# Placing the eight fetches of the next block's turned rows among the leaves of the second layer

## Chip, cores and metric

The kernel runs on one core of one Trainium2 chip. The metric is the device time of one execution in microseconds (us). TensorE (PE) does matmuls, VectorE (DVE), ScalarE (ACT) and GpSimd (POOL) do elementwise work, and SyncE (SP) issues nearly all DMA transfers from one queue in order. Each engine runs its own instructions in program order, and semaphores make it wait for data of other engines.

## The reference

Performer attention for 8 batches, 8 heads, 576 positions and 64 dimensions gives `x` of shape (8, 576, 512), and a Fourier mixing block with an MLP follows. All data is float32.

```python
X = np.fft.fft(x, axis=1)
X = np.fft.fft(X, axis=2)
mixed = np.real(X).astype(np.float32)
u = x + mixed
mu = np.mean(u, axis=-1, keepdims=True)
var = np.mean((u - mu) ** 2, axis=-1, keepdims=True)
un = (u - mu) / np.sqrt(var + 1e-06)
ch = np.maximum(un @ w_ch1, 0.0) @ w_ch2
return (u + ch).astype(np.float32)
```

`w_ch1` is 512 x 2048 and `w_ch2` is 2048 x 512. The 8 x 576 = 4608 rows of `u` are the tokens of the MLP.

## The kernel before

**Stages.** The first part of the program does attention and mixing and writes the rows `u` to memory (`us`). The first 512 tokens go through the MLP there, in 4 plain tiles. The other 4096 tokens are 8 blocks of 512 (j = 0 to 7), and the late part of the program is these 8 blocks. Each block has a first layer (`first_of`, matmuls at line 1310) and a second layer (`product_of`, matmuls at line 1490). Both use a recursive scheme with 7 products in place of 8 for a 2 x 2 split, so sums of operands are formed first: `tt` from the normalised rows (`block_norms`, line 1171), `hs` from the hidden rows (line 1377) and `sums` inside a product (line 1457).

**The second layer.** It runs seven products in the order `ORDER = (1, 2, 4, 5, 6, 7, 3)`, and each product has seven leaves in the order of line 1383, `PARTS = (1, 2, 5, 6, 3, 7, 4)`. A leaf is four float32 matmuls in the source, eight matmul instructions in the trace, and needs one tile `wl` of 256 KB that SyncE loads from the prepared weights `w2l` (`loads_w2`, line 1393). There are 12 `wl` buffers; 49 leaves make one second layer. What a leaf leaves in PSUM is saved by ACT or added by DVE, and these steps are named: `p1`, `p5`, `u2` are saved (line 1465), `c11`, `c12`, `c22` are added (line 1470), and `read` marks the last leaf of a product. Leaves 1, 2 and 4 multiply hidden rows (or `hs`) directly, leaves 5, 6, 3 and 7 multiply `sums`.

**The next block's rows.** While block j - 1 is in its first layer, the rows of block j are loaded, normalised (`norm_of`) and transposed in blocks of 32 on DVE (`by_blocks`); the transposed rows go to memory as `turned[j, h]`, for two halves h = 0 and 1. When block j - 1 has used its own normalised rows for the last time, their four buffers (`slab`) come free. Then `fetched(j, h, dst)` brings the turned rows back into `unT`: four DMAs of 128 KB for each half, each into 32 partitions (line 988). This happens for j = 1 to 7, so 56 fetches in all; block 0 takes another way, with transposes on PE. After the fetches `block_norms` forms the sums `tt`, four DVE instructions at line 1171, and the first layer of block j can begin when the second layer of j - 1 is nearly done.

**What sets the order.** The program is written out by a planner (`Listing.run`). Each stream of work (`late_turns`, `late_norms`, `halves`, `loads_w2`, `weight_sums`) yields `Step`s with an engine, an estimated time, events that must have been made before (`after`), an event that it makes, buffers that it takes and gives, and a `bias`. The planner always takes the step that could begin first by its own estimates, plus its bias, and emits its instructions. So an `after` event sets the place of an instruction in its engine's order. On the chip an instruction waits for what it reads and overwrites, and not for such an event by itself. For transfers the planner counts `kb` against a rate of 190 KB per us, and `late` as the delay from issue to landing. Here the fetch of a half is one `Step` of 1.7 us on SP that emits four DMAs in a row, as soon as the buffers are free and the turned rows are in memory.

Of the kernel before, what the change touches and what calls it, by code (L numbers as in the profile page):

```python
# [35 lines left out]
PE, ACT, DVE, POOL, SP, NONE = "pe", "act", "dve", "pool", "sp", "none"  # L36
# [244 lines left out]
def kernel(  # L281
# [39 lines left out]
    TB = 512  # L321
# [26 lines left out]
    mlpp = early.enter_context(tc.tile_pool(name="mlp", bufs=2))  # L348
# [612 lines left out]
    def events_of(tt):  # L961
        return tuple(sorted({("us", r // S) for t in tt for r in (P * t, P * t + P - 1)}))
# [4 lines left out]
    turned = {}  # L967
# [12 lines left out]
        nc.sync.dma_start(t[:, :, k], w[:].rearrange("p g d q -> p g (d q)"))  # L980

    def fetched(j, h, dst):
        yield Step(
            SP, 1.7, 3.0, after=(("turned", j, 2 * h), ("turned", j, 2 * h + 1)),
            makes=("unT", j, h), kb=330,
        )
        for g in range(4):
            nc.sync.dma_start(
                dst[Q * g : Q * g + Q].rearrange("q (b k) d t -> q b (k d t)", k=2),
                turned[j, h][:, g].rearrange("(b q) k n -> q b (k n)", q=Q),  # L990
            )
# [148 lines left out]
    def sums_right(b11, b12, b21, b22, t1, t2, t4):  # L1140

        return (
            (t1, b12, b11, ALU.subtract),
            (t2, b22, t1, ALU.subtract),
            (b12, b22, b12, ALU.subtract),
            (t4, b21, t2, ALU.subtract),
        )
# [3 lines left out]
    def block_norms(j, pool):  # L1151
        t0 = (NPLAIN * TP + TB * j) // 128
        yield Step(NONE, take=("slab",) * 4, after=events_of(range(t0, t0 + TB // 128)) + ("converted",))
        un = unTs[j] = [slabs.tile([128, HT // Q, NDC, Q], F32, name="unT2", tag="slab") for _ in range(2)]
        tt = [slabs.tile([128, 2, HT // Q, D2, Q], F32, name="tt", tag="slab") for _ in range(2)]
        tts[j] = tt[0][:, 0], tt[0][:, 1], tt[1][:, 0]
        for i in range(TB // 128):
            h, k = divmod(i, HT // 128)
            if pool is mlpp:
                dst = un[h][:, 4 * k : 4 * k + 4].rearrange("p g d q -> p d g q")  # L1160
                yield Fork(norm_of(j, t0 + i, i, pool, dst))
            elif not k:
                yield Fork(fetched(j, h, un[h]))
        parts = TB // 128 if pool is mlpp else 2
        yield Step(NONE, after=tuple(("unT", j, i) for i in range(parts)), bias=1.54)
        ops = sums_right(
            un[0][:, :, 0:D2], un[1][:, :, 0:D2], un[0][:, :, D2:NDC], un[1][:, :, D2:NDC], *tts[j]
        )
        for i, (o, l, r, op) in enumerate(ops):
            yield Step(DVE, 0.6, makes=("tt", j) if i == 3 else None, port=True, bias=-0.49)  # L1170
            nc.vector.tensor_tensor(out=o, in0=l, in1=r, op=op)
# [89 lines left out]
    def pairs(start):  # L1261
# [9 lines left out]
        [first(), loads(), loads_v(), load_tables(), frames(), plain_norms(), mixing()]  # L1271
        + [pairs(i) for i in range(NS)]
        + [w2_parts(), weight_sums((0,)), block_norms(0, mlpp), plain(), weights(), warm()],
        PICKS,
    )
# [317 lines left out]
    def late_norms():  # L1593
        for j in range(1, NTB):
            yield from block_norms(j, late)
# [36 lines left out]
```

## Time and profile before

| | us |
|---|---|
| median of 3 runs | 1165.73 |
| lowest and highest run | 1164.71, 1167.06 |
| the profiled execution | 1174.67 |
| its span, first to last instruction | 1172.2 |
| first layers of the blocks, one PE piece each of 168 matmuls | 36.26 |
| second layer of block 7, one PE piece of 368 matmuls | 41.10 |

The span is taken on the profiled execution, which is longer than the runs without a profile. PE stands for matmuls and PEld for TensorE's weight loads, which overlap them. "SPq" is SyncE's queue of DMA issues. In waits, "A <- B: 3.1, 5, 1.4" says that A waited for B for 3.1 us in total, 5 times, 1.4 us at most. In the chain of waits the work that ended last is followed back from the end: a piece "DMA wl<-w2l" goes from the issue of a load to its landing, and the instruction after it was released by that landing. The late part begins at about 424 us in the span, and a block takes about 93 us of it.

### The profile page before, as it was taken

To read this page: it belongs to the slowest core of one execution; us is meant where nothing else is said; L and a number is where in the kernel's file an instruction comes from. 1 tells how busy PE (TensorE), PEld (TensorE's weight loads), DVE (VectorE), ACT (ScalarE), POOL (GpSimd) and SP (SyncE) were. 2 spreads that over 40 slices of the span, in tenths; PEclk is the share of its full clock that TensorE was granted. 3 is DMA by queue.
4 is the path that set the end of the run, shared out by engine and by line. 5 is a ranking of instruction groups with operands and counts; after the bars stand their busy time and mean duration, and the time that the engine had idled before them with its cause. 6 is when DMAs were issued, how large, how long until landed. Compare 5 with 4: busy or idle time off the path is not lost.

```text
span 1172.2 us, 31328 instructions
## 1 busy us (share of the span) xinstructions
PE 1153.5 (98%) x12437; PEld 1032.9 (88%) x12437; DVE 754.7 (64%) x1573; ACT 436.8 (37%) x1485; POOL 430.4 (37%) x496
## 2 busy tenths in 40 slices
PE   8999999999999999999999999999999999999998
PEld 7888888779777868998998998898999899899898
DVE  5999999986676655744754664573573574474255
ACT  6998898866444212122112212212212212221211
POOL 2433444455472106225225324413513512522421
PEclk8999999999999999999999999999999999999999
DMA  7866765665662254873783593694495396388055
GB/s 218 224 188 186 240 181 178 203 210 163 207 196 101 77 162 139 263 264 85 222 278 112 172 308 99 152 317 141 112 319 190 82 290 231 83 258 263 35 166 203
DMA packets 167217, 220.34 MB, mean 188 GB/s; under 512 B 50080, under 2 KB 81056, under 8 KB 167072
## 3 DMA queue, kind: packets, MB, share of 16 engines
q1 hardware_dynamic: 166576, 218.09, 60.7%
q8 instruction: 98, 1.61, 0.6%
q14 instruction: 47, 0.39, 0.1%
q10 hardware_dynamic: 496, 0.26, 0.1%
HBM read 179.24 MB, written 43.25 MB: 190 GB/s over the span
## 4 chain that ended last, share of the span: by engine, by line
PE 88%; DMA 5%; DVE 4%; ACT 2%; SPq 1%; issue 1%; DVEq 0%
PE banks L1310 33%; PE banks L1490 27%; PE banks L1099 5%; PE banks L606 5%; PE banks L1122 4%; PE banks L512 4%; DMA wl<-w2l 3%; PE banks L640 2%; PE banks L687 2%; PE banks L849 2%; PE banks L799 1%; ACT e L566 1%; DVE nmx L549 1%; DMA kq<-in_k_dram 1%; PE banks L809 1%; PE banks L860 1%
## 5 line engine op out<-in xcount | busy, mean ns | idle before, releaser
L1490 PE MATMUL banks<-wl,sums 128*128 128x128 f32 x1792 | 217.4, 275 | 0.0
L1490 PEld LDWEIGHTS banks<-wl,sums 128*128 128x128 f32 x1792 | 208.6, 192 | 0.0
L1296 DVE CUSTOM_DVE_ANT_0 hid<-banks,s 128x256 f32<-128x256 f32 x192 | 80.9, 424 | 188.8 <-PE banks L1310 188.8
L566 ACT ACTIVATE e<-banks,nmx 128x128 f32<-128x128 f32 x576 | 165.3, 434 | 23.2 <-DVE nmx L549 22.4
L1324 ACT ACTIVATE s<-banks 128x256 f32<-128x256 f32 x192 | 73.7, 384 | 259.0 <-PE banks L1310 259.0
L1310 PE MATMUL banks<-unT,w 128*128 128x256 f32 x704 | 166.3, 379 | 0.0
L1310 PEld LDWEIGHTS banks<-unT,w 128*128 128x128 f32 x704 | 133.2, 190 | 18.3 <-issue 0.5
L1530 POOL TENSOR_TENSOR ur<-ur,part 128x512 f32<-128x512 f32 x32 | 47.3, 1479 | 267.1 <-ACT part L1523 187.0
L1465 ACT ACTIVATE s<-banks 128x128 f32<-128x128 f32 x168 | 46.6, 278 | 256.7 <-PE banks L1490 220.3
L1310 PE MATMUL banks<-tt,w1s 128*128 128x256 f32 x512 | 126.3, 379 | 0.0
L1310 PEld LDWEIGHTS banks<-tt,w1s 128*128 128x128 f32 x512 | 97.0, 190 | 13.7 <-DVE hid L1296 0.4
L1490 PE MATMUL banks<-wl,hid 128*128 128x128 f32 x768 | 100.0, 276 | 3.2 <-DMA wl<-w2l 3.1
L1470 DVE TENSOR_TENSOR part<-banks,s 128x128 f32<-128x128 f32 x168 | 49.0, 292 | 83.4 <-PE banks L1490 82.2
L549 DVE TENSOR_REDUCE nmx<-banks 128x8 f32<-128x1024 f32 (+1 forms) x96 | 89.3, 951 | 19.7 <-PE banks L606 15.5
L1490 PEld LDWEIGHTS banks<-wl,hid 128*128 128x128 f32 x768 | 94.0, 192 | 6.0 <-DMA wl<-w2l 4.5
L606 PE MATMUL banks<-om,kqT 64*64 64x128 f32 (+1 forms) x2088 | 80.6, 278 | 1.9 <-ACT kv L656 1.2
L1310 PE MATMUL banks<-unT,w1s 128*128 128x256 f32 x320 | 79.5, 379 | 0.0
L606 PEld LDWEIGHTS banks<-om,kqT 64*64 64x64 f32 (+1 forms) x2088 | 65.8, 140 | 13.3 <-issue 4.3
L1490 PE MATMUL banks<-wl,hs 128*128 128x128 f32 x576 | 75.1, 275 | 0.5 <-DVE part L1470 0.4
L1490 PEld LDWEIGHTS banks<-wl,hs 128*128 128x128 f32 x576 | 70.1, 192 | 1.2 <-DVE part L1470 0.6
L1377 POOL TENSOR_TENSOR hs<-hid,hs 128x256 f32<-128x256 f32 x64 | 50.1, 784 | 57.2 <-issue 37.1
L1310 PEld LDWEIGHTS banks<-unT,w1s 128*128 128x128 f32 x320 | 60.4, 190 | 8.7
(128 smaller groups left out, 1914.6 us busy)
## 6 DMA issues: line engine op xcount, KB each, us to landing
wl<-w2l SPq DMA_DIRECT2D x392, 256.0 KB
raw<-in_moe_w_ch_dram SPq DMA_DIRECT2D x32, 512.0 KB
kq<-in_k_dram SPq DMA_DIRECT2D x32, 288.0 KB
kq<-in_q_dram SPq DMA_DIRECT2D x32, 288.0 KB
vd<-in_v_dram SPq DMA_DIRECT2D x32, 288.0 KB
u<-us SPq DMA_DIRECT2D x36, 256.0 KB
ur<-us SPq DMA_DIRECT2D x36, 256.0 KB
out_dram<-ur SPq DMA_DIRECT2D x34, 256.0 KB
```

Source lines behind the costliest of these rows:

```text
L512: nc.tensor.transpose(ps[:, (j - j0) * 128 : (j - j0 + 1) * 128], src(j), ident[:])
L549: nc.vector.tensor_reduce(nmx[:, :, 0:num], pps[:, :, 0 : MF * num].rearrange("p b (c m) -> p b c m", m=MF), axis=AX.X, op=ALU.max, negate ...
L566: nc.scalar.activation(out=e[:, c + (i if num == 1 else 0), :], in_=pps[:, i, MF * c : MF * c + MF], func=AF.Exp, bias=nmx[:, i, c : c + 1],)
L606: nc.tensor.matmul(pps[cols, c, MF * m : MF * m + MF], lhsT=kqT[rows, j, cols], rhs=om2[rows, :],)
L1099: nc.tensor.matmul(hp[:, 0:TP], lhsT=w1[:, dc, 128 * fc : 128 * fc + 128], rhs=unTs[key][:, dc, :], start=(dc == 0), stop=(dc == NDC - 1),)
L1296: nc.vector._custom_dve(TENSOR_ADD_SAT, out=o, in0=ps, in1=sb, s0=FMAX, s1=0.0)
L1310: nc.tensor.matmul(ps[:, 0:HT].rearrange("f (b q) -> f b q", q=Q), lhsT=left(dc), rhs=right(dc), start=start and dc == 0, stop=(dc == D2 - 1),
L1324: nc.scalar.activation(out=s[:], in_=ps[:, 0:HT], func=AF.Copy)
L1377: nc.gpsimd.tensor_tensor(out=o, in0=l, in1=r, op=op)
L1470: nc.vector.tensor_tensor(out=part[:, t, 128 * m : 128 * m + 128], in0=ps[:, 0:128], in1=saved[with_][:], op=ALU.add,)
L1490: nc.tensor.matmul(ps[:, 0:128], lhsT=left[:, f], rhs=wls[j, i, n][:, f], start=start and f == 0, stop=(f == 3), skip_group_check=True,)
L1530: eng.tensor_tensor(out=o, in0=o, in1=other, op=ALU.add)
```

## The change

Each of the four fetches of a half becomes a `Step` of its own, with its own event and with one more `after` event. For the first half these events are the first save, the second save, an addition and the last leaf of product 1 of the second layer of block j - 1; for the second half an addition, the third save and another addition of product 2, and the first save of product 4. The estimate of one fetch is 0.47 us on SP, 3.4 us until it has landed and 82 KB, where four together had 1.7 us, 3.0 us and 330 KB. The sums `tt` are planned after all eight events. The transfers themselves are not changed.

```diff
     def fetched(j, h, dst):
-        yield Step(
-            SP, 1.7, 3.0, after=(("turned", j, 2 * h), ("turned", j, 2 * h + 1)),
-            makes=("unT", j, h), kb=330,
-        )
-        for g in range(4):
+        at = ((1, "p1"), (1, "p5"), (1, "c12"), (1, "read")) if h == 0 else ((2, "c11"), (2, "u2"), (2, "c22"), (4, "p1"))
+        for g, (i, what) in enumerate(at):
+            yield Step(
+                SP, 0.47, 3.4,
+                after=(("turned", j, 2 * h), ("turned", j, 2 * h + 1), (("second", j - 1, i), what)),
+                makes=("unT", j, 4 * h + g), kb=82,
+            )
             nc.sync.dma_start(
                 dst[Q * g : Q * g + Q].rearrange("q (b k) d t -> q b (k d t)", k=2),
                 turned[j, h][:, g].rearrange("(b q) k n -> q b (k n)", q=Q),
...
-        parts = TB // 128 if pool is mlpp else 2
+        parts = TB // 128 if pool is mlpp else 8
         yield Step(NONE, after=tuple(("unT", j, i) for i in range(parts)), bias=1.54)
```

## The prediction

> **What bounds the kernel now.** I read the page first, then the chain of waits in order of time, then the waits of PE and of SyncE's queue, and at last timelines and stretches of one second layer.
>
> ```profile
> PE 1153.5 (98%) x12437; PEld 1032.9 (88%) x12437; DVE 754.7 (64%) x1573; ACT 436.8 (37%) x1485; POOL 430.4 (37%) x496
> ```
>
> PE is busy 98% of the span, so a change can gain only where PE stands still, or where its matmuls are spaced out. The chain shows where that is in the second layers:
>
> ```profile
> 567.09 1.80 PE banks L1490 x16
> 570.94 5.40 DMA wl<-w2l
> 576.39 32.42 PE banks L1490 x288
> ...
> 659.84 41.31 PE banks L1490 x368
> ...
> 1125.18 41.10 PE banks L1490 x368
> ```
>
> The columns are start, length and what ran. Block 7's second layer (1125.18) has no next block to fetch, and its 368 matmuls take 41.10 us without a break. I take that as the undisturbed length. From the first long L1490 piece to the next L1310 piece the other stages of this view last: block 0 474.35 to 516.06, 41.71; block 1 567.09 to 608.81, 41.72; block 2 41.31; block 3 752.18 to 794.55, 42.37; block 4 845.58 to 887.27, 41.69; block 5 938.30 to 981.11, 42.81; block 6 1032.14 to 1074.15, 42.01. Less 41.10 each that is 0.61 + 0.62 + 0.21 + 1.27 + 0.59 + 1.71 + 0.91 = **5.92 us**. The DMA pieces of the chain (5.40 here, 4.96 to 6.71 in six stages) are not lost time: they run under PE's own work, and only their last part is waited for. The waits say who is late:
>
> ```profile
> PE banks L1490 <- DMA wl<-w2l: 3.1, 5, 1.4
> ...
> PEld banks L1490 <- DMA wl<-w2l: 4.5, 7, 1.6
> ...
> SPq L1393 <- DMA unT<-turned: 9.5, 34, 0.6
> ```
>
> PE and its weight loads (which overlap) wait for a `wl` load, and SyncE's queue, which issues these loads, waits 34 times for a fetch to land before it can issue the next load. SyncE's timeline of block 1 shows why:
>
> ```profile
> 566.25 0.32 SPq L1393 DMA_DIRECT2D wl<-w2l  x1
> 566.62 1.85 SPq L988 DMA_DIRECT2D unT<-turned  x4
> 568.57 0.38 SPq L1393 DMA_DIRECT2D wl<-w2l  x1
> 569.05 1.80 SPq L988 DMA_DIRECT2D unT<-turned  x4
> 570.94 10.69 SPq L1393 DMA_DIRECT2D wl<-w2l  x14
> ```
>
> The load issued at 570.94, behind all eight fetches, is the one whose landing ends the stall before 576.39. Two things delay it: the issue of the fetches (1.85 + 1.80 us) and their bytes. The stretches of the same stage give the rates:
>
> ```profile
> 569.00:573.00 4.00, 4.00 (x38) 4.00 (x38) 4.00 (x7) 1.11 (x4) 0.49 (x1) 1.00 1.03 215
> ...
> 577.00:581.00 4.00, 4.00 (x38) 4.00 (x38) 3.28 (x7) 0.56 (x2) 0.00 (x0) 1.00 1.05 386
> ```
>
> After the bounds and the length come the busy us of PE, its weight loads, DVE, ACT and POOL; the last two columns are the busy share of the DMA engines and GB/s. The engines are full in both; with loads alone they move 386 GB/s, with fetches among them 215. The third-last column is the granted clock, 1.00 throughout, so the clock plays no part.
>
> **What the change does to each queue.** No instruction is added or removed: the 56 fetches stay 56 of 128 KB, on the same queue. What moves is their place in SyncE's order, and behind them the four DVE instructions at L1171. The new `after` events are places in the planner's order, not waits on the chip: a fetch still waits there only for its source, its destination and the queue.
>
> *SyncE.* The first fetch keeps its place, because the event (1,"p1") lies before the stage and the slabs come free only at its beginning. Seven fetches go behind later leaves. By block 1's PE timeline (a leaf is 8 matmuls, 40 in 4.63 us less the overlap, about 0.89 us, and the leaves of products 1, 2 and later 4 alternate) I put the events at some 3, 4, 7, 8, 12, 13 and 14 us after the stage begins. So load 15 (the one of 570.94) is issued when its buffer comes free, the end of the fourth leaf, about 568.9, which is 2.0 us earlier. Load 14 comes 0.5 us earlier. Seven fetch issues of 0.45 us go between loads that are needed only some 9 us after their issue. In that window this queue holds nothing but loads; the stores come at the stage's end.
>
> *DMA time.* A load of 262 KB at 386 GB/s takes 0.68 us. A fetch alone is not shown. From below it costs 131 KB at 386 GB/s, 0.34 us. From above: from the issue of load 13 (566.25) to the landing of load 15 (576.34) there are 10.1 us, less three loads, over eight fetches, 1.0 us. I take 131 KB at 215 GB/s, 0.61 us, since that stretch is mostly fetches. In the new order at most two fetches stand ahead of load 15 in place of eight: 6 x 0.61 = 3.7 us less of queue (2.0 with the lower price, 6.0 with the upper). With the earlier issue it lands 4.0 to 8.0 us sooner than now; the greatest whole loss of one stage is 1.71. The stall is gone at every price.
>
> Over the 13.4 us of the first fifteen leaves the engines must now carry fifteen loads and eight fetches: 10.2 + 4.9 = 15.1 us (12.9 to 18.2). A backlog of 1.7 us (none to 4.8) grows slowly, and twelve buffers of 0.89 us stand against it. Leaves after that use 0.89 us for 0.68 of load, so it drains 0.2 us a leaf.
>
> A rule of the Trainium skill speaks against sending the fetches singly: "SBUF — State Buffer", section "The DMA setup-cost knee", gives every DMA some 2 us that do not depend on its size and advises the largest transfers. By that page's formula my estimate for one fetch is 2.3 us and for eight 18.4 us, instead of 4.9; here 14 loads are issued in 10.69 us, one in 0.76, so the trace does not bear it out where DMAs overlap.
>
> *VectorE.* The four L1171 instructions (the timeline of block 3 has them at 763.72 to 766.5, 0.69 us each, 2.75 in all) need all eight fetches. Now they run 12 us after their stage begins, in a stretch where DVE has slack; then they come when the last fetch is planned to land, 14 + 0.5 + 3.4 to 5 us, some 19 us after the stage's beginning. Their users, the next block's first matmuls with `tt`, start 42 us after it, so 20 us of cover are left. What they may push aside on DVE is the work of the fourth product:
>
> ```profile
> 769.78 0.68 DVE L1457 TENSOR_TENSOR sums<-hs 128x512 f32<-128x512 f32 x1
> ...
> 774.04 1.76 DVE L1457 TENSOR_TENSOR sums<-hs 128x512 f32<-128x512 f32 x1
> ```
>
> These feed leaves 5, 6, 7 and 3 of product 5. In the stretches of 4 us of this block DVE is busy 3.04 us from 768 and 3.90 from 772, then 2.63 and 2.04. So up to 2.75 us of delay is worked off by about 780. PE has three products open at a time, and leaves 1 and 2 of the next ones need no sums: three to four leaves, 2.7 to 3.6 us, can stand in. Cost on the path: nothing by that cover, up to 2.75 - 0.89 = 1.9 us a stage without it. I book 0.1 us a stage, 0.7 in all, for PE's order shifting around them.
>
> *The sum.* Gain between 4.0 us (what the stages lose over the best fetching one, 41.31: 5.92 - 7 x 0.21 = 4.45, less the 0.40 of block 0, whose late load belongs to a later product) and 5.92; I take 5.1, less 0.7 for DVE: **4.4 us**. The profiled execution took 1174.67 us, of which 1172.2 are span; it would become 1170.3 and 1167.8. It is 8.9 us longer than the median of the runs shown, 1165.73. The part that I change is a sum of waits, not a share of the whole, so I take the same 4.4 us off the median: **1161.3 us**.
>
> **The rivals.**
>
> *The wait moves to a later load.* Block 0 is the example: its stall before 489.02 ends with a load issued at 482.18 that took 6.71 us, long after the fetches were issued. If every stage kept such a loss (0.61 x 7 = 4.3 us), 1.6 us would be gained: 1164.1. Also, the profiled execution may stall more than the others do. For it: the backlog is spread, not removed. Against: the total queue ahead of such a load is smaller, since two or three fetches now come after it.
>
> *Slower: the L1171 group lands on DVE's full stretch.* The place is 19 to 22 us into the stage. It decides as soon as the last fetch's planned landing falls after the sums of product 5 are due and PE has no leaf without sums. The price is 1.9 us x 7 = 13.0 less the 4.4 gained plus the 0.7 already booked: +7.9, 1173.6. For it: 3.90 of 4 us busy, and the planner weighs those four ahead of the sums (bias -0.49 against -0.39). Against: no PE wait for sums now, and the planner can put other leaves there.
>
> *A single fetch is dear.* At 1.0 us or more each, fetches keep the loads from the engines for 8 us in 13, and the early loads of product 4 are late again by about 1 us in each stage: 7 us instead of 5.92, 1166.8. The fixed cost of the page named above would work in this direction. Against it stand the 14 loads in 10.69 us.
>
> *The change does nothing:* the loads in between hold the queue up so that the fetches still bunch. Then it is 1165.7. I count it with the first rival.
>
> **How the numbers follow.** Three runs spread over 0.2%, so 0.2% (2.3 us) is what a measurement can tell from no change. My forecast has a chance of 0.57, its own range 1159.0 (everything gained and a little more order) to 1163.3. The moved wait has 0.19, the dear fetch 0.04: both within 0.2%. The DVE collision, or another unlucky order of the planner of the same kind, has 0.20; half of it, at a smaller price than the full 1.9 us a stage, ends below 1170. So faster 0.57, same 0.23, slower 0.20. The range 1159.0 to 1170.0 leaves out the dear half of the last case and a little at each end of the first.
>
> **What would show it.** Right: SyncE's timeline has fetches singly between loads over some 13 us; the chain has no `wl` pieces in the second layers; PE's wait for `wl` falls below 1 us; the seven stages last 41.1 to 41.4 us; L1171 sits some 19 us into each stage and PE waits for no `sums`. Wrong: stages that still last over 41.6 with a `wl` load named (moved wait), PE waits at L1490 for `sums` or `part` (collision), or a first layer that starts late for `tt`.

## The result and the profile after

The changed kernel takes 1196.63 us (median of 6 runs, 1191.39 to 1198.82), the kernel before 1166.04 us beside it (6 runs, 1164.71 to 1167.06). The ratio is 1.0255, with a 95% interval from 1.0229 to 1.0281: 30.6 us slower. The prediction said 1161.3. The profiled execution after has a span of 1195.8 us. Lines of the source are two further down after the change (1490 is now 1492, 1171 is 1173).

The page's first line after, and then the chain of waits in order of time (start, length, what ran) for blocks 1 and 7:

```profile
PE 1160.4 (97%) x12437; PEld 1042.1 (87%) x12437; DVE 763.5 (64%) x1587; ACT 435.6 (36%) x1485; POOL 408.6 (34%) x482
```

```profile
563.91 14.72 PE banks L1492 x132
578.63 8.00 DMA wl<-w2l
...
586.77 23.30 PE banks L1492 x192
...
1149.01 41.10 PE banks L1492 x368
```

PE does the same 12437 matmuls; against the profiled execution before (span 1172.2 us) it is busy 7 us longer and stands still for some 17 us more. Block 7, which fetches nothing, is as it was, 41.10 us. Each of the seven others is now cut by one load that takes 5.87 to 8.12 us from issue to landing, in all seven the 29th load of the block, that of leaf 1 of product 6. The early stalls, which the change was to remove, are gone: the first matmul after a stall is now 23.3 to 25.7 us into the stage, where it was 8 to 17 us. (Here and below a stage is counted from the block's second leaf, 561.99 in block 1; that is 1.8 us before the first long L1492 piece, from which the prediction counts.) The waits (total, times, longest) say what it costs:

```profile
PEld banks L1492 <- DVE tt L1173: 21.9, 7, 4.3
...
PE banks L1492 <- DMA wl<-w2l: 20.8, 7, 4.2
...
DVE tt L1173 <- DMA wl<-w2l: 9.0, 5, 3.2
```

Before, PE's line had 3.1 us, and the weight loads waited 4.5 us for `wl`. The two lines with `tt` are new: the profile puts the same seven stalls of the weight loads down to `tt`, and VectorE itself stands there. That makes VectorE a second candidate for the cause. `tt` reads only fetched rows, so the `wl` in its line is no more than the landing that the profile saw last. SyncE's queue waits less for fetches and more for loads:

```profile
SPq L1395 <- DMA wl<-w2l: 27.0, 39, 2.5
...
SPq L1395 <- DMA unT<-turned: 3.2, 12, 0.6
```

Before, these were 9.9 and 9.5 us. SyncE's timeline of block 1 shows what stands ahead of that load:

```profile
570.57 0.42 SPq L990 DMA_DIRECT2D unT<-turned  x1
571.09 0.38 SPq L1395 DMA_DIRECT2D wl<-w2l  x1
571.51 0.43 SPq L990 DMA_DIRECT2D unT<-turned  x1
572.04 3.84 SPq L1395 DMA_DIRECT2D wl<-w2l  x5
575.93 1.72 SPq L990 DMA_DIRECT2D unT<-turned  x3
578.14 13.30 SPq L1395 DMA_DIRECT2D wl<-w2l  x12
```

Five fetches go singly, but the last three come in a row, since their events, (1,"read"), (2,"c22") and (4,"p1"), lie close together. By their semaphores those three landed 8.0 to 8.7 us after their issue, where the first one took 3.1 us and the planner counts with 0.47 + 3.4. The load issued at 578.63, behind them and one more load, is that of leaf 1 of product 6. PE would have used it at 583.6, 4.9 us after its issue (4.1 to 4.9 us in the seven stages): the planner, which gives a load 2.6 us to land, had taken this leaf forward.

The stall is not all. PE's timeline of block 1 (start, length, how many matmuls, idle time before):

```profile
582.51 1.06 PE L1492 MATMUL banks<-wl,sums 128*128 128x128 f32 x8
586.77 1.13 PE L1492 MATMUL banks<-wl,hs 128*128 128x128 f32 x8 [3.20 <-DMA wl<-w2l]
587.73 1.65 PE L1492 MATMUL banks<-wl,sums 128*128 128x128 f32 x8
589.17 1.91 PE L1492 MATMUL banks<-wl,hs 128*128 128x128 f32 x8
```

Eight matmuls that took 1.06 us ahead of the stall take 1.65 and 1.91 us behind it. Stretches of the trace laid on the clock's record (bounds, length, busy us of PE, its weight loads, DVE, ACT and POOL, granted clock, DMA share, GB/s) show why:

```profile
588.03:591.44 3.41, 3.41 (x18) 3.41 (x18) 0.99 (x4) 0.46 (x2) 0.00 (x0) 0.50 0.86 308
...
779.18:786.01 6.83, 5.27 (x25) 5.30 (x26) 3.19 (x5) 0.55 (x2) 0.00 (x0) 0.50 0.79 248
```

The granted clock is half of full speed for 3.41 us, or twice that, behind six of the seven stalls: four times 3.41 and twice 6.83, 27.3 us in all. PE is busy in 24.9 us of them, and at half speed half of that, 12.5 us, is lost. Read off the chain, the seven pieces of 192 matmuls behind the stalls are together 13.5 us longer than 21.44 us each, which is 192/368 of block 7's stage. In the kernel before the clock was whole in these stages. So the account is: 20.8 us of waits + 13.5 us of slower matmuls - 5.9 us of early stalls gone = 28.4 us; the seven stages together are 28.35 us longer.

### The profile page after: what moved, and what is told of

Its sections match the earlier page's. It is cut to its first block, busy times and chain, and to the rows that moved or that the text cites. A ratio compares the mean times of both kernels' runs of the same rounds, so it can differ in the third digit from the quotient of the medians.

```text
span 1195.8 us, 31327 instructions
## 1 busy us (share of the span) xinstructions
PE 1160.4 (97%) x12437; PEld 1042.1 (87%) x12437; DVE 763.5 (64%) x1587; ACT 435.6 (36%) x1485; POOL 408.6 (34%) x482
## 4 chain that ended last, share of the span: by engine, by line
PE 89%; DMA 6%; ACT 2%; DVE 1%; SPq 1%; issue 0%; DVEq 0%; ACTq 0%
PE banks L1312 32%; PE banks L1492 28%; PE banks L1101 5%; PE banks L606 5%; PE banks L512 5%; DMA wl<-w2l 4%; PE banks L1124 4%; PE banks L640 2%; PE banks L687 2%; PE banks L849 2%; PE banks L799 1%; ACT e L566 1%; PE banks L809 1%; PE banks L860 1%; DMA kq<-in_q_dram 1%; PE banks L695 1%
## 5 line engine op out<-in xcount | busy, mean ns | idle before, releaser
L1492 PE MATMUL banks<-wl,sums 128*128 128x128 f32 x1792 | 224.0, 279 | 0.0
L1492 PEld LDWEIGHTS banks<-wl,sums 128*128 128x128 f32 x1792 | 214.9, 196 | 0.0
L1532 POOL TENSOR_TENSOR ur<-ur,part 128x512 f32<-128x512 f32 x18 | 25.6, 1425 | 316.3 <-DVE part L1532 291.5
L1312 PEld LDWEIGHTS banks<-tt,w1s 128*128 128x128 f32 x512 | 97.0, 190 | 13.6 <-DVE hid L1298 0.3
L1492 PE MATMUL banks<-wl,hs 128*128 128x128 f32 x576 | 83.7, 293 | 21.2 <-DMA wl<-w2l 20.8
L1492 PE MATMUL banks<-wl,hid 128*128 128x128 f32 x768 | 100.1, 275 | 0.0
L1492 PEld LDWEIGHTS banks<-wl,hs 128*128 128x128 f32 x576 | 77.3, 207 | 22.9 <-DVE tt L1173 21.9
L1492 PEld LDWEIGHTS banks<-wl,hid 128*128 128x128 f32 x768 | 94.7, 192 | 1.2
```

The costliest lines, as they stand in the source:

```text
L1312: nc.tensor.matmul(ps[:, 0:HT].rearrange("f (b q) -> f b q", q=Q), lhsT=left(dc), rhs=right(dc), start=start and dc == 0, stop=(dc == D2 - 1),
L1492: nc.tensor.matmul(ps[:, 0:128], lhsT=left[:, f], rhs=wls[j, i, n][:, f], start=start and f == 0, stop=(f == 3), skip_group_check=True,)
```

## The experiments

The account leaves open why the load is late, and whether the clock is a cause at all. Runs of one batch are compared with the kernel before on the same chip: 1167.76 us for the first four, 1167.77 for the next four, 1169.28 (12 runs) for the third batch, 1169.72 (29 runs) for the last. Times of the first eight, and of e9_early, e10_burst_late and e12_last_early, are single runs. "Halved" in the tables is the time in the second layers for which the clock's record stands at half.

### First batch: what makes the load late

Theories: P, two of the three fetches in a row write the same quarter of the partitions; S, three in a row are too many; V, it is not the load but VectorE, which stands at `tt` until the fetches land and holds back the work behind it; D, the fetches' pieces in memory of 1 KB are dear. In the expectations, B holds that the DMA engines are by then behind with every load.

e1_halves, the second half's quarters in another order:

```diff
-        for g, (i, what) in enumerate(at):
+        for n, (i, what) in enumerate(at):
+            g = (n + 2 * h) % 4
```

> The order of the four fetches of the second half is 2, 3, 0, 1 instead of 0, 1, 2, 3, so that the last three fetches of a stage, which stand together in SyncE's queue, no longer go all into partitions 64 to 127. Theory P (the three late fetches crowd one half of the partitions, and the loads that write there too are held up): PE's wait for wl falls from 20.8 us to below 8 and the time to about 1175. Theory B (it is their bytes at a moment when the DMA engines have no slack) and theory V (the four L1173 instructions block VectorE until the last fetch has landed): both expect no change, 1190 to 1199.

e2_tt_late, the sums `tt` planned only after product 5 has been read:

```diff
-        yield Step(NONE, after=tuple(("unT", j, i) for i in range(parts)), bias=1.54)
+        later = () if pool is mlpp else ((("second", j - 1, 5), "read"),)
+        yield Step(NONE, after=tuple(("unT", j, i) for i in range(parts)) + later, bias=1.54)
```

> Fetches as in the changed kernel, but the four tt instructions on VectorE are planned after the last leaf of product 5, some 27 us into the stage, when the fetches have long landed. Theory V: most of the loss goes, 1166 to 1172, and VectorE no longer waits at L1173 for a fetch. Theories P and B: VectorE's wait goes, but PE still waits for wl for some 15 to 20 us in total; 1185 to 1197.

e3_apart, the last fetch of each half moved off the others:

```diff
-        at = ((1, "p1"), (1, "p5"), (1, "c12"), (1, "read")) if h == 0 else ((2, "c11"), (2, "u2"), (2, "c22"), (4, "p1"))
+        at = ((1, "p1"), (1, "p5"), (1, "c12"), (1, "c22")) if h == 0 else ((2, "c11"), (2, "u2"), (2, "c22"), (4, "u2"))
```

> The last fetch of the first half follows c22 of product 1 and the last of the second half u2 of product 4, so that no two fetches are issued one right after the other. Theory S (the loss comes from three fetches in a row, 14 us into the stage): 1164 to 1172, PE's wait for wl below 5 us. Theory B (single fetches between loads cost the loads more than a bunch does, wherever they stand): 1185 to 1197. Theory V: about as now, since tt still waits for the last landing.

e4_rows, the same bytes fetched from contiguous rows, so that the rows come in another order than the kernel needs:

```diff
-                dst[Q * g : Q * g + Q].rearrange("q (b k) d t -> q b (k d t)", k=2),
-                turned[j, h][:, g].rearrange("(b q) k n -> q b (k n)", q=Q),
+                dst[Q * g : Q * g + Q].rearrange("q b d t -> q (b d t)"),
+                turned[j, h][Q * g : Q * g + Q].rearrange("q a k n -> q (a k n)"),
```

> Each fetch reads 32 whole rows of the turned tile, 4 KB in one piece for a partition, instead of a quarter of each of 128 rows, 1 KB pieces; bytes, places and partitions written are the same, the rows are in another order than the computation wants. Theory D (the loss comes from the pieces of 1 KB, which take the engines as long as pieces of 2 KB): a fetch costs half, PE's wait for wl falls below 8 us, 1166 to 1176. Theories P, S and V: no change beyond 5 us, 1188 to 1199.

| | time, us | PE's waits for `wl`: total, times, longest | halved, us |
|---|---|---|---|
| changed kernel, profiled | 1198.82 | 20.8, 7, 4.2 | 27.3 |
| e1_halves | 1184.40 | 15.2, 7, 3.0 | 10.2 |
| e2_tt_late | 1198.01 | 17.6, 7, 3.3 | 27.3 |
| e3_apart | 1184.87 | 14.3, 7, 3.9 | 6.8 |
| e4_rows | 1189.31 | 15.5, 7, 2.8 | 13.7 |

V falls: with `tt` out of the way no DVE wait for a fetch is left and the time stays. P, S and D each take 7 to 12 us off the change's median, and none removes the stall: all seven waits stay in all of them. D expected a fetch to cost half in e4_rows; the eight fetches of block 1 took 59.5 us of packet time on the DMA engines there and 71.1 us in the change, 16% less. Much of what they save is clock and not wait. In e1_halves the waits fall by 5.6 us and the halved time by 17.1 us, worth 8.5. So a small change of a landing is made larger by the clock, and these three runs can't rank P, S and D against each other.

### Second batch: the planner's prices

e5_wl_late tells the planner that a load lands 5.5 us after its issue instead of 2.6; e6_old_wl_late does the same in the kernel before; e7_kb counts a fetch as 165 KB instead of 82; e8_hold holds leaf 1 of product 6 until product 5 has come to its step u2. U in the expectations holds that the stalled load is used too soon after its issue.

```diff
# e5_wl_late, and e6_old_wl_late in the kernel before
-                        SP, 0.45, 2.6, take=("wl",), after=(("w2l", i),), kb=165, makes=("wl", j, i, l)
+                        SP, 0.45, 5.5, take=("wl",), after=(("w2l", i),), kb=165, makes=("wl", j, i, l)
# e7_kb
-                makes=("unT", j, 4 * h + g), kb=82,
+                makes=("unT", j, 4 * h + g), kb=165,
# e8_hold
-        xb, x = yield from leaf(1, None, a(0, 0), True, ready(0), take=one)
+        held = ((("second", j, 5), "u2"),) if i == 6 and j < NTB - 1 else ()
+        xb, x = yield from leaf(1, None, a(0, 0), True, ready(0) + held, take=one)
```

> The changed kernel, but the planner counts 5.5 us from the issue of a wl load to its landing instead of 2.6, so that PE's order uses every load later. Theory U: the wait for wl below 8 us, 1166 to 1176. Theory B: as changed, 1185 to 1198.

> The kernel before with the same 5.5 us for a wl load. Theory U holds for its short stalls too (they are at leaf 1 of product 4, used 5 us after its issue): PE's wait for wl goes below 1 us, 1160 to 1165. If those stalls come from DMA engines that are behind with every load, no gain: 1165 to 1170.

> The changed kernel, but the planner counts a fetch as 165 KB, as it does a wl load, instead of 82. Theory U, in the form that the planner's price of a fetch is too low for what it costs the loads behind it: PE's order puts leaf 1 of product 6 and the tt instructions some 4 us later, the wait for wl falls below 8 us, 1166 to 1178. Theory B: 1185 to 1198.

> The changed kernel, but leaf 1 of product 6 in the blocks before the last is planned after u2 of product 5, some 2.2 us or two to three leaves later in PE's order. Theory U (PE's order takes the load of that one leaf 5 us after its issue, and it lands 8 us after it): PE's wait for wl falls from 20.8 us to below 8, the granted clock shows at most two halvings in the second layers, 1168 to 1176. Theory B (the DMA engines are behind with all loads by then): the wait moves to the next leaf and stays over 15 us, 1185 to 1198.

| | time, us | PE's waits for `wl` | halved, us | PE's other new waits |
|---|---|---|---|---|
| e5_wl_late | 1185.31 | 7.3, 7, 1.5 | 0 | ACT `s`: 6.0, 11, 0.6 |
| e6_old_wl_late | 1173.16 | 2.1, 3, 0.9 | 0 | DVE `sums` 1.1, POOL `hs` 1.1 |
| e7_kb | 1183.10 | none | 0 | "issue": 12.1, 7, 1.7; ACT `s` 2.4 |
| e8_hold | 1184.25 | 12.0, 6, 2.8 | 3.4 | "issue": 1.8, 6, 0.6 |

Where the planner counts loads or fetches as dearer, the waits for loads shrink or go, and so does the halved clock. That speaks for a load that is used too soon. But U was right for the waits alone, and only in e5_wl_late and e7_kb; the times that it expected (1166 to 1178 us, and 1160 to 1165 for e6_old_wl_late) were all too low. None of these is near the kernel before, and a dearer load makes that kernel 5.4 us slower too: a leaf that is moved away from its load is moved into another wait. In e8_hold the leaf comes later and the wait stays at 12.0 us, because its load is still behind the last fetches: issued at 582.78, it needs 6.00 us.

e7_kb shows a cost that the prediction had named. Its PE timeline of block 1 has a new gap of 1.72 us with no load behind it:

```profile
591.73 1.95 PE L1492 MATMUL banks<-wl,sums 128*128 128x128 f32 x16
595.40 1.13 PE L1492 MATMUL banks<-wl,sums 128*128 128x128 f32 x8 [1.72 <-issue]
```

The profile names no releaser for it. DVE's timeline of the same time has the four instructions of `tt` (two are shown) ahead of sums that are done at 595.30, just before this leaf starts:

```profile
588.65 0.69 DVE L1173 TENSOR_TENSOR tt<-unT,unT 128x512 f32<-128x512 f32 x1
...
590.67 0.68 DVE L1173 TENSOR_TENSOR tt<-unT,tt 128x512 f32<-128x512 f32 x1
...
592.20 1.43 DVE L1459 TENSOR_TENSOR sums<-sums,hid 128x512 f32<-128x512 f32 x1
593.55 1.75 DVE L1459 TENSOR_TENSOR sums<-hs,sums 128x512 f32<-128x512 f32 x1
```

So I put the gaps down to `tt`, by these times alone. With the waits for `s`, PE loses 12.1 + 2.4 = 14.5 us, 2.1 us a stage, and the kernel is 15.3 us above the one before.

### Third batch: the place in the stage against singleness

These four replace the line of the fetches' events, or in the kernel before that of the bursts. In the expectations, L holds that the late place of the last three fetches is what costs, N that fetches between loads are dear wherever they stand.

```diff
# e9_early, in the changed kernel
+        at = ((1, 'p1'), (1, 'c11'), (1, 'p5'), (1, 'u2')) if h == 0 else ((2, 'c11'), (2, 'p5'), (4, 'p1'), (2, 'u2'))
# e12_last_early, in the changed kernel
+        at = ((1, 'p1'), (1, 'p5'), (1, 'c12'), (1, 'c12')) if h == 0 else ((2, 'c11'), (2, 'u2'), (2, 'u2'), (4, 'p1'))
# e10_burst_late, in the kernel before
-            SP, 1.7, 3.0, after=(("turned", j, 2 * h), ("turned", j, 2 * h + 1)),
+            SP, 1.7, 3.0, after=(("turned", j, 2 * h), ("turned", j, 2 * h + 1), (("second", j - 1, 1), "read")),
# e11_loads_first, in the kernel before
+            SP, 1.7, 3.0, after=(("turned", j, 2 * h), ("turned", j, 2 * h + 1), (("second", j - 1, 2 - h), ("c11", "p5")[h])),
```

> The change with all eight single fetches due within some 8 us of the start of the stage (the fetches of the first half after p1, c11, p5 and u2 of product 1, those of the second after c11 and p5 of product 2, p1 of product 4 and u2 of product 2). Theory L (what costs is that three fetches stand in the queue at 14 to 16 us, right ahead of the loads that product 6's leaf 1 uses some 5 us after their issue): the fetches are down long before, TensorE's waits for loads of these stages fall from 20.8 us to under 5, no clock halving is left behind them, and the time is 1164 to 1172 us. Theory N (single fetches between loads are dear wherever they stand): a stall of 2 us or more moves to another leaf of each stage, the waits stay over 10 us and the time is 1180 us or more.

> The kernel before, its two bursts of four fetches kept, but both held until product 1 has been read, some 12.5 us into the stage instead of at its start. Theory L: the loads of product 6's leaf 1 come down behind eight fetches; a stall of 3 us or more in each of the seven stages, the clock halved behind most, 1185 us or more. Theory N: bursts are as cheap there as at the stage's start, no stall over 2 us, 1164 to 1170 us.

> The kernel before with its two bursts of four, each let pass by the loads of product 4's first leaves: the first half's burst waits for c11 of product 2, the second half's for p5 of product 1 (some 2 us later than before). Theory L: nothing stands ahead of the loads of product 4's leaf 1 nor of product 6's, the old stalls (5.9 us in all seven stages) are gone and no new one comes: 1160 to 1165 us. If the old stalls came from the transfers that share the engines and not from the order in the queue, they stay at their size and the time is 1165 to 1170 us. Theory N says as the latter.

> The change with only its last three fetches moved: the fourth of the first half stands beside its third (after c12 of product 1), and the third and fourth of the second half after u2 of product 2 and p1 of product 4, so that all are issued some 5 to 7 us sooner; the first five stay. Theory L: as with all eight early, waits for loads under 5 us, no halving, 1164 to 1173 us. Theory N: no better than the runs that thinned or spread the last three (1184 to 1185 us).

| | time, us | PE's waits for `wl` | halved, us | last fetch issued, us into the stage |
|---|---|---|---|---|
| e9_early | 1176.12 | 6.1, 8, 1.5 | 0 | 10.2 to 11.0 |
| e10_burst_late | 1189.44 | 15.1, 7, 2.5 | 10.2 | 17.7 to 19.2 |
| e11_loads_first | 1174.68 (10 runs), 1.0047 [1.0032, 1.0063] | 5.1, 5, 1.5 | 0 | 7.4 to 8.3 |
| e12_last_early | 1168.76 | 2.1, 3, 1.2 | 0 | 10.5 |

The two runs that set the theories apart are e12_last_early and e10_burst_late. The first keeps five fetches where the change has them and only brings the last three forward. SyncE's timeline of its block 1:

```profile
567.18 3.00 SPq L1395 DMA_DIRECT2D wl<-w2l  x4
570.23 2.32 SPq L990 DMA_DIRECT2D unT<-turned  x5
572.65 8.91 SPq L1395 DMA_DIRECT2D wl<-w2l  x11
```

Five fetches now stand in a row, and the time is that of the kernel before: three in a row are not what costs by themselves. The second takes the old bursts and moves them, all eight, to 14 us into the stage and later:

```profile
569.49 13.01 SPq L1393 DMA_DIRECT2D wl<-w2l  x14
582.55 4.86 SPq L988 DMA_DIRECT2D unT<-turned  x8
587.51 10.39 SPq L1393 DMA_DIRECT2D wl<-w2l  x13
```

With no single fetch in it, it has the stall (seven times, at the load of the same leaf, 24 to 25 us into the stage) and in three stages the halved clock; it loses 20.2 us. So late fetches cost in rows as they do singly, as L says. The mechanism is not quite the change's: here the load lands in 4.2 to 5.2 us, no longer than in the kernel before, but the fetches hold its issue back until 2.0 to 3.2 us before PE could use it.

The two runs differ from their parents in the leaves' order too, since the planner orders them by the same events. In blocks 0 to 3 of e12_last_early the load of leaf 1 of product 6 lands 5.0 to 5.1 us after its issue, and the first leaf that could use it starts 7.6 us or more after it. So place and order are not told apart. e16_second_burst below keeps the leaves' order, but tests an early place alone.

L was too hopeful elsewhere. e9_early, expected at no more than 1172 us, has stalls of 0.3 to 1.5 us at some 18 us in six stages. In e11_loads_first the stalls move from the loads of product 4's first leaves to one behind the eight fetches, 0.6 to 1.5 us in five stages, and it is slower than the kernel before. There the load behind eight fetches in a row pays for them.

### Fourth batch: the clock, and the best place

e13_idle_filled tests the clock by itself. It leaves the fetches and the order as the change has them, and gives PE twelve matmuls of no use while it waits; their result is overwritten by the leaf.

```diff
+            for f in range(12 if (i, n) == (6, 1) and j < NTB - 1 else 0):
+                nc.tensor.matmul(
+                    ps[:, 0:128],
+                    lhsT=left[:, f % 4],
+                    rhs=left[:, f % 4],
+                    start=True,
+                    stop=True,
+                    skip_group_check=True,
+                )
```

> The change, with twelve matmuls of no use (2.7 us at the 224 ns of one) put ahead of leaf 1 of product 6 in the seven stages, into the bank that the leaf then starts afresh. The loads come when they came, so TensorE's leaf starts no sooner. Theory C (the clock is halved because TensorE stood idle): the halvings behind these stalls are gone, the 13.7 us that they cost are won back, less 1 to 2 us in the two stages where the wait was shorter than 2.7 us: 1184 to 1188 us, 10 us or more faster than the change though it does more work. Rival (the halvings have another cause, or what they cost is hidden by the loads that follow): they stay, or go without a gain, and the time is 1195 to 1202 us.

It takes 1186.63 us (4 runs, 1184.96 to 1190.54), 10.0 us less than the change. Each against the kernel before beside it, it loses 16.9 us (1.0147 [1.0120, 1.0174]) where the change loses 30.6. Its chain of waits and a stretch of its block 1 (its leaves are line 1501, the added matmuls line 1492):

```profile
566.40 19.65 PE banks L1501 x176
586.05 2.68 PE banks L1492 x24
588.73 21.44 PE banks L1501 x192
```

```profile
588.00:592.00 4.00, 4.00 (x38) 4.00 (x37) 2.89 (x6) 0.55 (x2) 0.00 (x0) 1.00 0.97 299
```

No load stands in the chain of block 1, since PE is busy until it lands, and the 192 matmuls behind it take 21.44 us instead of 23.30. The clock is whole in all seven stages. Doing 18.8 us more matmuls won back 10 to 14 us: the halved clock is a cause, and PE's idleness is what brings it.

The last three look for the best place; e14_again is e12_last_early once more.

```diff
# e15_pairs, in the changed kernel
+        at = ((1, "p1"), (1, "p1"), (1, "p5"), (1, "p5")) if h == 0 else ((1, "c12"), (1, "c12"), (2, "c11"), (2, "c11"))
# e16_second_burst, in the kernel before
+            SP, 1.7, 3.0, after=(("turned", j, 2 * h), ("turned", j, 2 * h + 1)) + ((("second", j - 1, 2), "c11"),) * h,
```

> The kernel of e12_last_early once more, timed in five rounds. Theory L (the place of the last three fetches is what costs): its stages keep 2 us of waits for loads where the kernel before has 3 to 5, so it stands 0 to 3 us (up to 0.25%) below the kernel before. If the single run was a lucky one, it stands 2 us or more above it.

> The change with its fetches in four pairs, two after each of p1, p5 and c12 of product 1 and c11 of product 2, so that the last is issued some 9 us into the stage instead of 16. Theory L: no stall over 1.5 us anywhere, waits for loads under 3 us in all, 0 to 5 us below the kernel before. Theory N (fetches between loads are dear in themselves): no better than all eight early (1176 us).

> The kernel before with the first burst of four where it was and the second held until c11 of product 2 has been written, some 4 us later than it was; TensorE's order is that of the kernel before. Theory L: the loads of product 4's first leaves have only one burst ahead of them, the early stalls of 1 us and more are gone, and no leaf behind the second burst is used within 5 us of its load: 0 to 5 us below the kernel before. Rival: the second burst makes a stall of its own at product 4's last leaves or product 5's first, and the time is 0 to 5 us above it.

| | time, us (12 runs each) | ratio to the kernel before, 95% | PE's waits for `wl` |
|---|---|---|---|
| e14_again | 1167.77 | 0.9985 [0.9970, 1.0001] | 1.7, 3, 0.7 |
| e15_pairs | 1168.16 | 0.9988 [0.9973, 1.0003] | 1.2, 2, 0.6 |
| e16_second_burst | 1168.12 | 0.9987 [0.9972, 1.0002] | 2.4, 4, 0.9 |

e16_second_burst is the plainest of them: PE's order is that of the kernel before, and only the second burst stands lower in SyncE's queue. It is lower by one load and 0.4 us, where some 4 us were expected.

```profile
561.59 1.85 SPq L988 DMA_DIRECT2D unT<-turned  x4
563.53 0.85 SPq L1393 DMA_DIRECT2D wl<-w2l  x2
564.43 1.85 SPq L988 DMA_DIRECT2D unT<-turned  x4
566.38 13.82 SPq L1393 DMA_DIRECT2D wl<-w2l  x17
```

All three end 1.6 to 2.0 us below the kernel before, each with an interval that just reaches 1. That is the size L expected, and at the edge of what twelve runs can tell; none is shown to beat the kernel before.

## Why the prediction was wrong

**The early stalls.** Right in kind: with seven fetches moved out of the way, the loads of product 4 landed in time and no stall was left there. Wrong in size: the sum counted 5.1 us from one profiled execution that was 8.9 us above the median. The three kernels that end those stalls and bring few new ones stand 1.6 to 2.0 us lower, which is not clear of no gain.

**The step that failed: "Seven fetch issues of 0.45 us go between loads that are needed only some 9 us after their issue."** That holds for the leaves that are used in the order of their loads. In the seven stages of the change the load of leaf 1 of product 6 was needed 4.1 to 4.9 us after its issue, and behind the last three fetches it takes 5.87 to 8.12 us. The place of the last three was right (some 12, 13 and 14 us, against 12.2, 13.0 and 13.6 in block 1, counted as the prediction does), but the text spoke of fetches one at a time and did not ask which load stands behind each, and when that one is used. "The stall is gone at every price" was true of load 15 (the 16th of a block, since the prediction counts from 0) and did not reach the 29th.

**The DMA backlog.** That "twelve buffers of 0.89 us stand against it" was the wrong cover: buffers give time only to a load that is used in turn. That fetches and loads together overfill the engines was seen, and the price of a fetch was near: the packets of block 1's eight fetches are 0.56 us each on 16 engines, against 0.61. The backlog of 1.7 us was mis-sized. From issue to landing, as a mean of the seven stages, the 14th load of a block takes 2.8 us, the 22nd 5.7, the 27th 8.0 and the 29th 7.4; in the kernel before these are 3.0, 5.4, 5.4 and 4.9. Nor did it drain by 0.2 us a leaf: from 571 to 579 us in block 1 the engines moved 320 GB/s, by which a load takes some 0.8 us of a leaf's 0.89 (an estimate, since two fetches are in that stretch).

**The clock.** That "the clock plays no part" was read from a kernel whose stages lose at most 1.7 us each. It is some 13 us of what was lost, and with the wait filled 10 to 14 us came back.

**The rivals.** "The wait moves to a later load" is what happened, at 3.0 us a stage (20.8 / 7) where 0.61 was taken from block 0, and without the clock; with both it would have stood well above the kernel before. Spoken against it was that two or three fetches come after such a load; all eight were ahead of this one. "Slower: the L1171 group" was not the cause here, as the run with `tt` planned later shows; its mechanism and price, 1.9 us a stage, fit what was seen in e7_kb, 2.1. "A single fetch is dear" did not decide. With the last fetch issued by some 12 us into the stage, five in a row and pairs cost nothing; eight singly cost 7 us (e9_early, one run) and eight in a row 5 (e11_loads_first). Late ones, from 14 us on, cost 31 us in the change and 20 in e10_burst_late.

**What held.** Block 7 is unchanged at 41.10 us. The first layers keep their 36.26 us, so `tt` is in time for them. The fixed cost of a transfer that the Trainium skill gives ("SBUF — State Buffer", section "The DMA setup-cost knee") was left out of the sum, and that did no harm. By the estimate made from it there, eight fetches cost 18.4 us a stage; e14_again sends three singly and five in a row, and its time is that of the kernel before.

**What stays open.** Why the last fetches need 8 us is not settled. Writing other quarters, contiguous rows and a wider spread each took some of the wait, and none was tried with the others. A rival that no run tests stands in the trace. A transfer tells of its landing by 16 updates of its semaphore, and in the seven stages the last update for the stalled load came 0.05 to 2.4 us behind the 15th, 8.5 of the 20.8 us in all. In block 1 this begins with the load issued at 573.77, ahead of the last three fetches: its 15th update comes at 578.97, its last at 581.62, and the next two loads too take over 8 us. A packet of 16 KB of the page's queue "q8 instruction" (98 in the span) starts at 577.94. The kernel before has such late updates too, so part of the stall may be instructions that are fetched at a bad moment. That the planner moved leaves in nearly all of these runs limits what each of them says alone.

## What to carry to other kernels

Before moving a transfer down a queue, list the loads that will stand right behind it, with the time from each one's issue to its use: here the shortest of these decided, not the average and not the number of buffers. When transfers are spread by events, look at where the events fall in time, since two that fall together make a row again. And a stall of a few microseconds on TensorE should be priced with the clock behind it: here seven stalls of 1.7 to 4.2 us cost two thirds more than their own length.

## What the runs showed of the hardware

The halved stretches begin on a grid of 3.413 us: in the change, 588.03 and 683.60 are 28 such steps apart. I laid that grid through the second layers of the traces of both kernels and of eleven experiments, and took PE's busy share of each step that was not halved itself. All 20 steps with a share of 0.41 or less were followed by a halved one; of four between 0.43 and 0.46 three were; of the steps from 0.47 up none was. So a stall's length alone does not decide. One of 1.84 us in the change brought the halved clock on, and gaps of 2.8 us in e8_hold that lay across two steps did not.

The Trainium skill, "TensorE: Matmul & The Clock Gate", section "Part 1: The HAM clock gate", has such a window of 3413 ns that runs by itself, and lets the clock fall to half after an idle window. The traces agree on the window and on the half. They differ on what counts as idle: TensorE was busy for up to 0.46 of the step before a halved one. The advice in that page's section "Why this matters for your kernels", no gap over some 3 us, would have let stalls of 1.84 to 2.8 us pass that halved the clock here.

A second thing: a busy share of the DMA engines is no rate. It stood at 1.06 to 1.10 from 571 to 583 us in block 1 of the change, while they moved 320 GB/s up to 579, mostly loads, and 238 GB/s behind that, when the three fetches came through.
